# New landing delays in a planner's DMA model, and new orders and placements for attention followed by an MoE layer, on one core

## The chip, the cores and the metric

The kernel runs on one core of a Trainium2 chip. The metric is the device time of one execution in microseconds (us); where several executions were timed, their median is given. The core has five engines with an instruction queue each: TensorE (PE, with its weight loads PEld), VectorE (DVE), ScalarE (ACT), GpSimd (POOL) and SyncE (SP), which here issues every DMA. Each engine works through its own queue in order; engines wait for each other by semaphores.

## What is computed

The input is q, k and v of 4 batches, 8 heads, 576 positions and 64 dimensions, and two weights. Attention is the sum of two parts, one over means of four positions, one over a band of seven:

```python
q_d = q.reshape(B, H, Sd, factor, D).mean(axis=3)   # factor = 4, k_d and v_d alike
out_d = sm_attn(q_d, k_d, v_d)
out_up = np.repeat(out_d, factor, axis=2)
mask = np.abs(pos[:, None] - pos[None, :]) < factor
scores = np.where(mask, scale * np.matmul(q, k.transpose(0, 1, 3, 2)), -1000000000.0)
...
out_local = np.matmul(attn, v)
return (out_up + out_local).astype(np.float32)
```

Its result, as x of 2304 tokens by 512, goes through a layer with weights of 512 by 2048 and 2048 by 512:

```python
h = x @ w_in
sp = np.where(h > 20.0, h, np.log1p(np.exp(np.minimum(h, 20.0))))
g = h * np.tanh(sp)
return (g @ w_out).astype(np.float32)
```

## The kernel before

Attention is cut into 16 units, one for each batch b and pair p of heads (`attention`, line 399; "unit 2_1" is batch 2, pair 1). A unit loads qk (line 417, 582 KB) and vv (line 503, 1152 KB). DVE sums qk over four positions (line 418), PE makes coarse scores (line 433) and banded scores (line 472), ACT takes the exponentials (lines 440 and 482 or 492), DVE divides by their sums. POOL sums v over four positions (lines 506 and 508). PE transposes the probabilities (lines 517, 518, 551) and multiplies them with the sums of v (lines 538 and 542) and with v (line 566). DVE adds both parts into x32 (line 579).

The MoE layer works on 384 tokens (c, six of them) and 128 columns of w_in (f, sixteen of them). Tokens of c = 0 and 1 are split into two float32r parts in SBUF and go through 32 "slots" (line 773): four times three matmuls into h (line 785), then `tail` (line 791): Mish on ACT (line 809), a split into two parts (lines 812 to 815), and nine matmuls into the accumulators (line 828). Tokens of c = 2 to 5 go to DRAM (far, line 592), come back as sums (line 646) and operands (line 666, tile q), and go through 16 "quartets" (line 723), which form four products of two c and two f out of seven smaller ones (line 746). A weight (line 614) comes as raw 64-bit numbers (512 KB each for wi and wo), is converted on ACT and DVE (lines 630 to 634) and split (lines 638 to 641).

The first four units (batch 0) run in a prologue with three buffer sets of their own and a fourth that is shared; matmuls on the identity (line 927, "warm") fill PE's gaps there. All later units share the one set "att", whose buffers exist once: a buffer goes to the next unit in program order when the one before is through (`turn`, lines 82 and 214). The quartets' operands lie in that set too (lines 674, 675 and 707 to 714).

The order of instructions is not written out. Every operation is recorded with an engine, a duration, what it reads and writes, and a priority (a low number is urgent). `Plan.order` (line 173) then plays the whole program through: each time an engine is free by its clock, it gets the most urgent operation whose inputs are there. What comes out is the fixed order of each engine's queue. For SP (lines 270 to 273) it has a model of when a DMA lands: `o.dur` is bytes over 415 GB/s, `dma` the end of what was queued before.

The constants at the top set priorities and choices: ATT (base and step for each batch) with UNIT (one unit) give a unit's priority, ATT[b][0] + ATT[b][1] * p + UNIT; slots have their number s, 0 to 31, and quartets start at 32. LAG puts the second product behind s (three values: s < 20, < 60, above). WPRI (base, step for each f, extra for wo), WACT and WDMA belong to weights, SPRE, SPRE2, JPRE and XDMA to sums, QPRE, QPRE2, QDMA to operands, TPRE and UPRE to quartets, VOFF to vv's DMA; STICK and KEEP make PE and ACT stay with matmul shapes and function tables. AMUL, AEXP, WHI, RDV and GHI list the units, weights and slots for which a step is done on ACT or on DVE: a unit in AMUL normalises on ACT (line 448), else on DVE (line 451); in AEXP it takes nine exponentials with their sums on ACT (line 482), else one, with DVE passes around it (lines 490 to 493); in RDV it spreads the rest of the coarse part on DVE (line 524), else with three ACT operations (line 530).

Of the kernel before, what the change touches and what calls it, by code (L numbers as in the profile page):

```python
# [19 lines left out]
P = 128  # L20
BIG = 1e30
CH = 384
LAG = (0.33, 3.75, 19.55)
FA = 5
SETS = 3
ATT = {0: (-845.5, 70.5), 1: (0.3, 1.8), 2: (-2.6, 0.3), 3: (-13.3, 4.2)}
WPRI = (1.59, 11.3, 10.35)
UNIT = {(0, 0): -48, (1, 3): -18, (0, 3): 15, (1, 2): -6, (0, 2): 17, (1, 1): -23, (0, 1): 65, (1, 0): 8, (3, 3): 14, (2, 3): -12, (3, 2): 5, (2, 0): -3, (2, 2): 6, (3, 0): -11, (2, 1): -3, (3, 1): -23}
WARM = True
NPRO = 4  # L30
WACT = 95
STICK = 71
VOFF = 12
WDMA = -72
PIPE0 = (1, 0, 1)
PIPE1 = (1, 0, 1)
LEAD = 3
PMASK = (0, 1)
AMUL = ((0, 2), (0, 3), (1, 0), (1, 1), (1, 3))
AEXP = ((0, 2), (1, 2))  # L40
WHI = ((0, 'wo'), (4, 'wo'), (7, 'wi'), (8, 'wi'), (12, 'wi'), (12, 'wo'), (13, 'wo'), (14, 'wo'), (15, 'wo'))
RDV = ((0, 1), (0, 2), (0, 3), (1, 3), (2, 2), (2, 3), (3, 0), (3, 1), (3, 2))
GHI = (9, 10, 11, 13, 14, 15, 18, 21, 22, 24, 25, 29, 31)
NMISH = (4,)
TAIL = 0
SPRE = 39
SPRE2 = 77
JPRE = -42
XDMA = -35
QPRE = 26  # L50
QPRE2 = 101
QSTEP = 0.6
QDMA = 93
SUMS = 2
TPRE = 82
UPRE = -19
KEEP = 94
LOAD, PRE = 1320, 250
TICK, BUSY, PACE = 3413.3, 3900, 4900
KW = 38  # L60
RATE, LAND = 415.0, 1100
PAGE, FIRST, FETCH = 256, 193, (2800, 5500)
DQ = 2500
# [33 lines left out]
class Plan:  # L97
# [6 lines left out]
    def buf(self, group, tag, shape, dtype=F32, bufs=1, name=None):  # L104
        return Buf(self, group, tag, shape, dtype, bufs, name or f"{tag}_{len(self.ops)}")
# [67 lines left out]
    def order(self):  # L173
# [10 lines left out]
        free = {"pe": 1500.0, "act": 1900.0, "dve": 0.0, "pool": 3290.0, "sp": 1080.0}  # L184
        dma, hot, parked, gap, look = 0.0, {0: 1000}, {}, 0, 0.0
# [4 lines left out]
        events, t, out = [0.0, *free.values()], 0.0, []  # L190
        while events:
            t = heapq.heappop(events)
            while events and events[0] <= t:
                heapq.heappop(events)
            for e in pending:
                while pending[e] and pending[e][0][0] <= t:
                    o = heapq.heappop(pending[e])[2]
# [4 lines left out]
                if e == "pe" and gap > 0 and ready[e]:  # L202
                    ready[e] = [(o.prio + (0 if o.gap else STICK), o.seq, o) for _, _, o in ready[e]]
                    heapq.heapify(ready[e])
                if e == "act" and ready[e]:
                    ready[e] = [(o.prio + (KEEP if o.tab and o.tab != tab else 0), o.seq, o) for _, _, o in ready[e]]
                    heapq.heapify(ready[e])
                while ready[e]:
                    item = heapq.heappop(ready[e])
                    o = item[2]  # L210
# [57 lines left out]
                        dur += max(0, lock["pool" if e == "dve" else "dve"] - t)  # L268
                        lock[e] = t + dur
                    if e == "sp":  # L270
                        late = t > 1e5
                        dma = max(dma, t + LAND + 400 * late) + o.dur * (1 + 0.28 * late)
                        free[e], end = max(t + 420, dma - DQ), dma + 600 * (late and o.dur < 800)
                    else:
                        free[e] = end = t + dur
                    o.end = end
# [22 lines left out]
                if e == "pe" and self.filler and free[e] <= t:  # L299
                    k = int(t // TICK)  # L300
                    o, when = None, max(1700, t + 120)
                    if 1700 <= t < 1e6 and self.load(t) < PACE:
                        o = self.fill(t)
# [23 lines left out]
def dve(n, fast=False):  # L327
    return 69 + (0.52 if fast else 1.042) * n


def act(n, psum=False, extra=0):
    return (52 if psum else 94) + 0.833 * n + 93 * extra
# [6 lines left out]
class Kernel:  # L339
# [59 lines left out]
    def attention(self, b, p, sb, ps, padded, loose):  # L399
# [45 lines left out]
        op("dve", 88, lambda: nc.vector.reciprocal(cst()[:, 3], cst()[:, 2]), w=[cst], two=False)  # L445
        if (b, p) in AMUL:
            for m in range(3):
# [14 lines left out]

        pmask = b in PMASK or (b, p) in AEXP

# [11 lines left out]
        wide = lambda i: lst()[:, i, :, None].broadcast_to([P, T, KW])  # L476
        if (b, p) in AEXP:
            op("dve", dve(T * KW), lambda: nc.vector.tensor_reduce(out=lst()[:, 0], in_=sl3(), op=ALU.max, axis=AX.X),
# [6 lines left out]
        else:  # L485
            if not pmask:
# [7 lines left out]
               r=[L], w=[lst], two=False)  # L494
        if (b, p) in AEXP:
            op("dve", 73, lambda: nc.vector.tensor_scalar(lst()[:, 1], lst()[:, 1], 1e-9, None, op0=ALU.add), r=[L], w=[lst])
# [3 lines left out]

        pv_ = pl.prio + VOFF
        vv, vd = buf("vv", [P, 18, P]), buf("vd", [P, 2, P])
# [12 lines left out]
        def tr():  # L515
# [6 lines left out]
            AT(), pa()[:, :384].rearrange("p (m h i) -> p h m i", m=3, h=2)[:, :, :, :48], AF.Copy), r=[pa], w=[AT])  # L522
        if (b, p) in RDV:
            op("dve", dve(288), lambda: nc.vector.tensor_tensor(
# [89 lines left out]
    def load_w(self, f):  # L614
# [6 lines left out]
        for nm, src in (("wi", wi), ("wo", wo)):  # L621
            pl.prio = prio + (WPRI[2] if nm == "wo" else 0)
            raw = pl.buf("wa" if f < FA else "wb", f"{nm}{f}", [P, 512, 2], I32, 1, f"raw_{nm}{f}")
# [4 lines left out]
            op("sp", P * 4096 / RATE, lambda raw=raw, src=src: nc.sync.dma_start(  # L628
                raw().rearrange("p (c f) w -> p c (f w)", c=4), src), w=[raw], prio=pl.prio + WDMA)
            op("act", act(512), lambda hi=hi: nc.scalar.activation(  # L630
                hi().bitcast(F32), hi().bitcast(F32), AF.Prelu, scale=2.0 ** -112, alpha=2.0 ** 32), w=[h], prio=pl.prio + WACT, tab="exp")
            op("dve", dve(512, True), lambda lo=lo: nc.vector.tensor_scalar(
# [3 lines left out]
               r=[l, h], w=[full])  # L636
            if (f, nm) in WHI:
                op("dve", dve(512, True), lambda w=w, full=full: nc.vector.tensor_copy(w()[:, 0], full()), r=[full], w=[(w, 0)])
# [7 lines left out]
    def sums(self, c):  # L646
# [4 lines left out]
        for j in range(2):  # L651
            pl.prio = (SPRE if c == 2 else SPRE2) + j * JPRE
            at = {}
            for k, (p, d) in raw.items():
                at[k] = b = pl.buf("stg", "stg", [P, 512], F32, self.nstg, f"s{k}{j}_{c}")
                x = self.far(p + j, c + d)
                op("sp", P * 4 * W / RATE, lambda b=b, x=x: nc.sync.dma_start(b()[:, :W], x()), r=[x], w=[b], prio=pl.prio + XDMA)
            for t, ko, a, b_, alu in ((1, "a22", "a21", "a22", ALU.add), (3, "a21", "a11", "a21", ALU.subtract),
# [4 lines left out]
                x = self.far("s", t, j, c)  # L663
                op("sp", P * 4 * W / RATE, lambda bo=bo, x=x: nc.sync.dma_start(x(), bo()[:, :W]), r=[bo], w=[x], prio=pl.prio + XDMA)

    def operands(self, c):
# [15 lines left out]
        for m, what in enumerate(("00", 2, "20", 3, 1, "21", 4)):  # L682
            for j in range(2):
                pl.prio = (QPRE if c == 2 else QPRE2) + m * QSTEP
                if isinstance(what, str):
                    p, d = int(what[0]) + j, int(what[1])
                    x, to = self.far(p, c + d), self.raw[p, d]
                else:
# [6 lines left out]
                op("sp", P * 4 * W / RATE, lambda b=b, x=x: nc.sync.dma_start(b()[:, :W], x()), r=[x], w=[b, (o, kh), (o, kl)],  # L695
                   prio=pl.prio + QDMA)
                op("act", act(W), lambda b=b, w=w: nc.scalar.activation(w()[:, 0], b()[:, :W], AF.Copy), r=[b], w=[(o, kh)])
# [25 lines left out]
    def quartet(self, s, i, c):  # L723
        nc, pl = self.nc, self.plan
        op = pl.op
        pl.prio = s + TPRE
        T = self.blocks(i)
# [24 lines left out]
        def plus(to, a, bank):  # L752
            op("dve", dve(CH), lambda: nc.vector.tensor_tensor(  # L753
                out=at[to](), in0=bank()[:, :CH], in1=at[a](), op=ALU.add),
               r=[bank] + u[a] * (a != to), w=u[to], prio=s + UPRE, two=False)

        bank = product(0, wt(w0, 0), xs(0, c))
        op("act", act(CH, True), lambda bank=bank: nc.scalar.activation(at["u1"](), bank()[:, :CH], AF.Copy),
           r=[bank], w=u["u1"], prio=s + UPRE)
        plus("u2", "u1", product(1, tt(2), ss(2)))  # L760
# [30 lines left out]
    def tail(self, s, c, f, h, own=None, place=("mish", "g"), last=None):  # L791
# [12 lines left out]
        for c0, c1, key in parts:  # L804
# [5 lines left out]
               r=h_, w=x_, tab="mish")  # L810
            if s in GHI:
                op("dve", dve(n, True), lambda o_=o_: nc.vector.tensor_copy(g()[:, 0, o_], Gv()[:, o_]), r=x_, w=[one])
# [10 lines left out]
        for i in range(3):  # L823
# [7 lines left out]
            gi = [g] if len(parts) == 1 else [(g, 2 * i), (g, 2 * i + 1)]  # L831
            op("pe", 700, mm2, r=[*gi, wo], w=[a_], cols=1536, prio=s + LAG[(s >= 20) + (s >= 60)] - 0.5 + 0.1 * i)
            if not last:
# [12 lines left out]
    def run(self, ctx):  # L846
# [29 lines left out]
        for b in (0, 1):  # L876
            for p in range(self.NPAIR):
                if len(units) == NPRO:
                    break
                units.append((ATT[b][0] + ATT[b][1] * p + UNIT.get((b, p), 0), self.attention(  # L880
                    b, p, sets[len(units) % len(sets)], ("props", "attps"),
# [4 lines left out]
        for f in range(self.NF):  # L886
            pl.prio = WPRI[0] + WPRI[1] * f
            self.load_w(f)
# [10 lines left out]
        def units(bs):  # L899
            us = [(ATT[b][0] + ATT[b][1] * p + UNIT.get((b, p), 0), self.attention(b, p, "att", "attps", probs["att"], False))  # L900
                  for b in bs for p in range(self.NPAIR) if 4 * b + p >= NPRO]
            self.record(us, PIPE1)
# [93 lines left out]
```

## Time and profile before

| what | value |
|---|---|
| median of 3 runs | 502.12 us (501.51 to 505.4) |
| the profiled execution | 505.01 us, its span 503.2 us |
| PE busy | 482.8 us (96%) |
| DVE, ACT, POOL busy | 360.8, 280.5, 40.8 us |
| DMA moved | 65.60 MB, mean 130 GB/s |
| mean granted clock of PE | 0.993 of full speed |
| chain that ended last | PE 79%, DMA 8%, ACT 7%, DVE 3%, POOL 2% |

All times inside the execution count from the start of its span. Busy means that the profile shows at least one instruction of the engine under way. A wait stands with the operation that it delayed, and names the engine, or the transfer, that ended it.

### The profile page before, as it was taken

How to read it: one execution, taken by the hardware profiler on the slowest of the kernel's cores; microseconds unless marked ns; L12 is line 12 of the kernel's file. 1: busy time of each engine (PE TensorE's matmuls, PEld its weight loads, DVE VectorE, ACT ScalarE, POOL GpSimd, SP SyncE). 2: the span in 40 equal slices, each digit the busy share in tenths (PEclk: the TensorE clock that was granted, in tenths of full speed). 3: DMA queues.
4: the chain of work that ended last, by engine and by line, in shares of the span. 5: the costliest groups of instructions: out<-in, count | busy, mean ns of one | idle time of the engine just before them, and what ended most of it. 6: DMA issues, size and time to landing. Idle time of an engine off the chain costs nothing.

```text
span 503.2 us, 11610 instructions
## 1 busy us (share of the span) xinstructions
PE 482.8 (96%) x4729; PEld 415.0 (82%) x4729; DVE 360.8 (72%) x818; ACT 280.5 (56%) x668; POOL 40.8 (8%) x70
## 2 busy tenths in 40 slices
PE   7998899989899999999999999999999999999996
PEld 3666788778788788888899999999889999888885
DVE  3999989979665778746896786667789976653511
ACT  2699899757485568675444333343566444333411
POOL 7401001011120111111000000000000000000000
PEclk9989899999999999999999999999999999999999
DMA  8967994314555478636210140100340000000003
GB/s 343 419 274 290 411 360 161 130 60 175 174 207 177 151 236 267 223 117 214 87 48 21 45 139 18 31 17 15 96 150 23 0 2 2 0 0 1 0 1 125
DMA packets 23381, 65.60 MB, mean 130 GB/s; under 512 B 2592, under 2 KB 12832, under 8 KB 21280
## 3 DMA queue, kind: packets, MB, share of 16 engines
q1 hardware_dynamic: 23328, 64.86, 35.9%
q8 instruction: 37, 0.61, 0.5%
q14 instruction: 16, 0.13, 0.1%
HBM read 53.84 MB, written 11.01 MB: 129 GB/s over the span
## 4 chain that ended last, share of the span: by engine, by line
PE 79%; DMA 8%; ACT 7%; DVE 3%; POOL 2%; issue 1%; POOLq 0%; SPq 0%
PE acc L828 35%; PE h L746 24%; PE h L785 9%; DMA vv<-in_vv_dram 4%; PE pve L566 2%; DMA raw_wi<-in_w_in_dram 2%; PE sc L433 2%; PE sl L472 2%; PE pt L551 1%; DMA far<-x 1%; PE pvo L538 1%; PE pvo L566 1%; POOL vv L506 1%; ACT raw_wi L630 1%; PE pvo L542 1%
## 5 line engine op out<-in xcount | busy, mean ns | idle before, releaser
L828 PE MATMUL acc<-wo,g 128*128 128x512 f32 x864 | 219.1, 395 | 0.5 <-ACT g L814 0.5
L828 PEld LDWEIGHTS acc<-wo,g 128*128 128x128 f32 x864 | 159.2, 188 | 30.0 <-ACT g L814 1.4
L753 DVE TENSOR_TENSOR u<-h,u 128x384 f32<-128x384 f32 x112 | 60.7, 554 | 30.4 <-PE h L746 27.9
L785 PE MATMUL h<-x,wi 128*128 128x384 f32 x384 | 76.6, 347 | 2.9 <-ACT mA L809 2.9
L785 PEld LDWEIGHTS h<-x,wi 128*128 128x128 f32 x384 | 67.8, 192 | 5.8 <-ACT mA L809 3.5
L809 ACT ACTIVATE u<-u 128x384 f32<-128x384 f32 (+1 forms) x66 | 33.8, 515 | 61.8 <-DVE u L753 61.6
L815 DVE TENSOR_TENSOR g<-u,g 128x384 fp32r<-128x384 f32 (+1 forms) x66 | 35.6, 544 | 38.5 <-ACT g L814 38.5
L814 ACT ACTIVATE g<-u 128x384 fp32r<-128x384 f32 (+1 forms) x66 | 33.5, 512 | 30.3 <-PE acc L828 29.4
L718 ACT ACTIVATE t<-b 128x256 fp32r<-128x256 f32 x64 | 26.3, 414 | 42.4 <-PE h L746 37.3
L746 PE MATMUL h<-x,wi 128*128 128x384 f32 x192 | 41.3, 338 | 0.0
L746 PE MATMUL h<-x,t 128*128 128x384 f32 x192 | 39.0, 338 | 0.6 <-DVE u L753 0.6
L506 POOL TENSOR_TENSOR vv<-vv 128x512 f32<-128x512 f32 x16 | 21.0, 1315 | 194.6 <-DMA vv<-in_vv_dram 166.3
L746 PEld LDWEIGHTS h<-x,wi 128*128 128x128 f32 x192 | 34.3, 188 | 1.6
L746 PEld LDWEIGHTS h<-x,t 128*128 128x128 f32 x192 | 33.8, 188 | 2.0 <-DVE u L753 1.2
L746 PE MATMUL h<-sfar,t 128*128 128x384 f32 x144 | 32.0, 340 | 0.1
L418 DVE TENSOR_REDUCE qkd<-qk 128x288 f32<-128x1152 f32 x16 | 21.4, 1340 | 13.4 <-DMA qk<-in_qk_dram 13.2
L719 DVE TENSOR_TENSOR t<-b,t 128x256 fp32r<-128x256 f32 x64 | 26.5, 418 | 4.0 <-ACT t L718 3.7
L746 PEld LDWEIGHTS h<-sfar,t 128*128 128x128 f32 x144 | 25.6, 188 | 3.5 <-DVE u L753 0.8
L715 DVE TENSOR_TENSOR b<-b,b 128x256 f32<-128x256 f32 x64 | 27.0, 423 | 1.0
L815 DVE TENSOR_TENSOR g<-mA,g 128x384 fp32r<-128x384 f32 x32 | 21.1, 665 | 8.7 <-ACT g L814 8.5
L709 DVE TENSOR_TENSOR b<-wi 128x256 f32<-128x256 f32 x64 | 25.8, 424 | 0.9 <-PE pvo L538 0.2
L566 PEld LDWEIGHTS pve<-PT,vv 38*64 38x64 f32 x640 | 21.1, 135 | 3.4 <-ACT PT L558 1.2
(116 smaller groups left out, 687.4 us busy)
## 6 DMA issues: line engine op xcount, KB each, us to landing
vv<-in_vv_dram SPq DMA_DIRECT2D x16, 1152.0 KB, 6.7
qk<-in_qk_dram SPq DMA_DIRECT2D x16, 582.0 KB, 6.6
raw_wi<-in_w_in_dram SPq DMA_DIRECT2D x16, 512.0 KB, 10.7
raw_wo<-in_w_out_dram SPq DMA_DIRECT2D x16, 512.0 KB, 10.4
out_dram<-o SPq DMA_DIRECT2D x18, 256.0 KB, 2.1
sa<-far SPq DMA_DIRECT2D x16, 192.0 KB, 2.8
fars<-sa SPq DMA_DIRECT2D x16, 192.0 KB, 2.8
q<-fars SPq DMA_DIRECT2D x16, 192.0 KB, 3.3
```

The source lines that it names most:

```text
L506: op("pool", gps(512), lambda: nc.gpsimd.tensor_tensor(out=vc()[:, :, 0:2], in0=vc()[:, :, 0:2], in1=vc()[:, :, 2:4], op=ALU.add), w=[(vv, ...
L566: nc.tensor.matmul(o_()[64 * h:64 * h + 64, c0:c0 + 32], vw()[64 * e:64 * e + KW, j, f, 64 * h:64 * h + 64], PT()[64 * e:64 * e + KW, j, 6 ...
L715: op("dve", dve(n), lambda ko=ko, a=a, b_=b_: nc.vector.tensor_tensor(out=t[ko](), in0=t[a](), in1=t[b_](), op=ALU.subtract), r=[t[a], t[b ...
L718: op("act", act(n), lambda w=w, ko=ko: nc.scalar.activation(w()[:, 0], t[ko](), AF.Copy), r=[t[ko]], w=[(w, 0)])
L719: op("dve", dve(n), lambda w=w, ko=ko: nc.vector.tensor_tensor(out=w()[:, 1], in0=t[ko](), in1=w()[:, 0].bitcast(F32), op=ALU.subtract), r ...
L746: nc.tensor.matmul(bank()[:, :CH], wv(a, j), xv()[:, b_], start=j == 0 and m == 0, stop=j == 1 and m == 2)
L753: op("dve", dve(CH), lambda: nc.vector.tensor_tensor(out=at[to](), in0=bank()[:, :CH], in1=at[a](), op=ALU.add), r=[bank] + u[a] * (a != t ...
L785: nc.tensor.matmul(h()[:, :CH], w()[:, a, kt * P:(kt + 1) * P], x()[:, b_, :], start=kt == 0 and j == 0, stop=kt == 3 and j == 2)
L809: op("act", act(n, psum), lambda o_=o_: nc.scalar.activation(Gv()[:, o_], Hv()[:, o_], AF.Mish), r=h_, w=x_, tab="mish")
L814: op("act", act(n), lambda o_=o_: nc.scalar.activation(g()[:, 0, o_], Gv()[:, o_], AF.Copy), r=x_, w=[one])
L815: op("dve", dve(n), lambda o_=o_: nc.vector.tensor_tensor(out=g()[:, 1, o_], in0=Gv()[:, o_], in1=g()[:, 0, o_].bitcast(F32), op=ALU.subtr ...
L828: nc.tensor.matmul(a_(), g()[:, a, i * P:(i + 1) * P], wo()[:, b_], start=first and j == 0, stop=last and j == 2)
```

## The change

Three lines of the planner's DMA model change, and constants at the top of the kernel. Before, a transfer had a start-up of 1100 ns up to 100 us of planned time and 1500 ns after; after 100 us its duration counted 1.28 times, and transfers priced below 800 ns (up to 256 KB) ended 600 ns later. Now the start-up is 1100 ns in the first 3 us and 1800 ns from then on; from 70 us the duration counts 1.28 times, and the 600 ns are added below 800 ns and above 2500 ns, which is vv. The constants give other priorities to units, weights, sums, operands and second products, and other choices between ACT and DVE. No operation is added or taken out but for those choices; the matmuls stay the same.

```diff
--- before.py
+++ after.py
@@ -20,41 +20,41 @@
 P = 128
 BIG = 1e30
 CH = 384
-LAG = (0.33, 3.75, 19.55)
+LAG = (0.1, 6.06, 26.18)
 FA = 5
 SETS = 3
-ATT = {0: (-845.5, 70.5), 1: (0.3, 1.8), 2: (-2.6, 0.3), 3: (-13.3, 4.2)}
-WPRI = (1.59, 11.3, 10.35)
-UNIT = {(0, 0): -48, (1, 3): -18, (0, 3): 15, (1, 2): -6, (0, 2): 17, (1, 1): -23, (0, 1): 65, (1, 0): 8, (3, 3): 14, (2, 3): -12, (3, 2): 5, (2, 0): -3, (2, 2): 6, (3, 0): -11, (2, 1): -3, (3, 1): -23}
+ATT = {0: (-842.3, 62.6), 1: (2.8, 3.8), 2: (-7.2, 5.7), 3: (-35.9, 5.6)}
+WPRI = (-2.33, 7.84, 15.62)
+UNIT = {(0, 0): -55, (1, 3): -15, (0, 3): 10, (1, 2): -8, (0, 2): 23, (1, 1): -38, (0, 1): 67, (1, 0): 5, (3, 3): 8, (2, 3): -11, (3, 2): 0, (2, 0): 2, (2, 2): 12, (3, 0): 2, (2, 1): 5, (3, 1): -22}
 WARM = True
 NPRO = 4
-WACT = 95
-STICK = 71
-VOFF = 12
-WDMA = -72
+WACT = 184
+STICK = 34
+VOFF = 1
+WDMA = -65
 PIPE0 = (1, 0, 1)
 PIPE1 = (1, 0, 1)
 LEAD = 3
 PMASK = (0, 1)
-AMUL = ((0, 2), (0, 3), (1, 0), (1, 1), (1, 3))
-AEXP = ((0, 2), (1, 2))
-WHI = ((0, 'wo'), (4, 'wo'), (7, 'wi'), (8, 'wi'), (12, 'wi'), (12, 'wo'), (13, 'wo'), (14, 'wo'), (15, 'wo'))
-RDV = ((0, 1), (0, 2), (0, 3), (1, 3), (2, 2), (2, 3), (3, 0), (3, 1), (3, 2))
-GHI = (9, 10, 11, 13, 14, 15, 18, 21, 22, 24, 25, 29, 31)
+AMUL = ((0, 2), (1, 0), (1, 1))
+AEXP = ((0, 2),)
+WHI = ((0, 'wo'), (2, 'wo'), (7, 'wi'), (8, 'wi'), (11, 'wi'), (12, 'wi'), (14, 'wo'), (15, 'wi'), (15, 'wo'))
+RDV = ((0, 0), (0, 1), (0, 2), (0, 3), (1, 0), (1, 3), (2, 0), (3, 0), (3, 2), (3, 3))
+GHI = (9, 10, 12, 13, 14, 16, 17, 18, 20, 23, 24, 25, 30)
 NMISH = (4,)
 TAIL = 0
-SPRE = 39
-SPRE2 = 77
-JPRE = -42
-XDMA = -35
-QPRE = 26
-QPRE2 = 101
+SPRE = 44
+SPRE2 = 104
+JPRE = -45
+XDMA = -45
+QPRE = -15
+QPRE2 = 100
 QSTEP = 0.6
-QDMA = 93
+QDMA = 51
 SUMS = 2
-TPRE = 82
-UPRE = -19
-KEEP = 94
+TPRE = 92
+UPRE = -20
+KEEP = 121
 LOAD, PRE = 1320, 250
 TICK, BUSY, PACE = 3413.3, 3900, 4900
 KW = 38
@@ -268,9 +268,9 @@
                         dur += max(0, lock["pool" if e == "dve" else "dve"] - t)
                         lock[e] = t + dur
                     if e == "sp":
-                        late = t > 1e5
-                        dma = max(dma, t + LAND + 400 * late) + o.dur * (1 + 0.28 * late)
-                        free[e], end = max(t + 420, dma - DQ), dma + 600 * (late and o.dur < 800)
+                        late = t > 7e4
+                        dma = max(dma, t + (LAND if t < 3000 else LAND + 700)) + o.dur * (1 + 0.28 * late)
+                        free[e], end = max(t + 420, dma - DQ), dma + 600 * (late and (o.dur < 800 or o.dur > 2500))
                     else:
                         free[e] = end = t + dur
                     o.end = end
```

## Rows read from the trace of the kernel before

**Rows 1.** The page: the span, and busy time of each engine
```profile
span 503.2 us, 11610 instructions
...
PE 482.8 (96%) x4729; PEld 415.0 (82%) x4729; DVE 360.8 (72%) x818; ACT 280.5 (56%) x668; POOL 40.8 (8%) x70
```

**Rows 2.** Busy us by stretch: PE, PEld, DVE, ACT, POOL; clock, DMA share, GB/s
```profile
0.00:42.00 42.00, 35.91 (x813) 23.36 (x813) 32.74 (x80) 26.38 (x91) 15.26 (x46) 0.96 0.81 318
42.00:110.00 68.00, 61.95 (x599) 52.70 (x597) 60.50 (x132) 58.80 (x139) 6.57 (x6) 0.97 0.67 257
110.00:242.00 132.00, 128.16 (x2042) 109.98 (x2042) 95.28 (x215) 86.33 (x201) 18.97 (x18) 1.00 0.55 185
242.00:499.70 257.70, 256.82 (x1293) 228.99 (x1285) 172.24 (x396) 108.64 (x238) 0.00 (x0) 1.00 0.12 37
```

**Rows 3.** Groups by line and shape, PE: the filler
```profile
L927 PE MATMUL warm<-ident 128*128 128x512 bf16 x32 | 11.3, 471 | 1.6 <-POOL ident masks.py:199 1.6
```

**Rows 4.** Timeline of PE: waits between 100 and 242 us, idle before in brackets
```profile
106.15 0.31 PE L518 MATMUL at<-ident,Ar_att 128*96 128x128 f32 x1 [1.63 <-DVE Ar_att L454]
...
138.79 0.47 PE L538 MATMUL pvo<-AT,vd 128*64 128x144 f32 x4 [1.67 <-POOL vd L508]
...
165.40 0.47 PE L538 MATMUL pvo<-AT,vd 128*64 128x144 f32 x4 [0.74 <-POOL vd L508]
...
233.24 2.33 PE L785 MATMUL h<-x,wi 128*128 128x384 f32 x12
...
237.82 0.47 PE L538 MATMUL pvo<-AT,vd 128*64 128x144 f32 x4 [0.89 <-POOL vd L508]
```

**Rows 5.** Timeline of DVE around 105 us
```profile
104.63 1.35 DVE L418 TENSOR_REDUCE qkd<-qk 128x288 f32<-128x1152 f32 x1 [3.11 <-DMA qk<-in_qk_dram]
...
105.90 0.20 DVE L454 TENSOR_TENSOR Ar_att<-A,cst 128x48 f32<-128x48 f32 x1
```

**Rows 6.** Timeline of SyncE's DMA queue: when four transfers were issued
```profile
95.31 0.33 SPq L503 DMA_DIRECT2D vv<-in_vv_dram  x1
...
97.84 0.33 SPq L417 DMA_DIRECT2D qk<-in_qk_dram  x1
...
128.67 0.33 SPq L503 DMA_DIRECT2D vv<-in_vv_dram  x1
...
227.80 0.33 SPq L503 DMA_DIRECT2D vv<-in_vv_dram  x1
```

**Rows 7.** Chain that ended last: start us, us, what; two transfers of vv
```profile
128.67 7.51 DMA vv<-in_vv_dram
...
156.10 6.99 DMA vv<-in_vv_dram
```

**Rows 8.** Timeline of POOL: sums of v behind two transfers
```profile
136.67 1.27 POOL L506 TENSOR_TENSOR vv<-vv 128x512 f32<-128x512 f32 x1 [12.29 <-DMA vv<-in_vv_dram]
...
138.01 0.72 POOL L508 TENSOR_TENSOR vd<-vv 128x256 f32<-128x256 f32 x1
...
235.68 1.29 POOL L506 TENSOR_TENSOR vv<-vv 128x512 f32<-128x512 f32 x1 [16.73 <-PE h L785]
```

**Rows 9.** DMA issues between 100 and 240 us: KB each, median us to landing
```profile
vv<-in_vv_dram SPq DMA_DIRECT2D x9, 1152.0 KB, 6.0
```

**Rows 10.** Groups by line, DVE and ACT: busy us, mean ns, idle before
```profile
L493 DVE TENSOR_REDUCE lst<-L_att 128x9 f32<-128x351 f32 x14 | 7.2, 511 | 0.0
...
L451 DVE TENSOR_TENSOR A<-A,cst 128x384 f32<-128x384 f32 x11 | 6.1, 554 | 0.1
...
L524 DVE TENSOR_TENSOR R_att<-at,diag 96x288 f32<-96x288 f32 x9 | 4.1, 451 | 2.0 <-ACT AT L521 1.8
...
L448 ACT ACTIVATE A<-A,cst 128x128 f32<-128x128 f32 x15 | 5.2, 398 | 0.2 <-DVE cst L445 0.2
...
L482 ACT ACTIVATE L_att<-sl,lst 128x38 f32<-128x38 f32 x18 | 5.2, 300 | 0.7 <-DVE lst L480 0.6
```

**Rows 11.** Waits of PE: us in total, times, longest
```profile
PE h L785 <- ACT mA L809: 2.9, 2, 2.3
```

## The prediction

> **What bounds the kernel now.** I read the page's first part, then the busy times by stretch, then the waits of TensorE (PE) in order of time, and then went back from each wait to the transfer behind it. PE is busy for 482.8 of 503.2 us; no other engine is above 72% [rows 1]. The stretches say where the other 20.4 us are [rows 2]: 6.1 in the first 42 us, where PE waits on chains of VectorE (DVE) and ScalarE (ACT) and partly runs filler; 6.05 between 42 and 110; 3.8 between 110 and 242; 0.9 in all of the last dense part up to 499.7; and 3.5 after PE's last instruction, for the last output. So the second half (the quartets) can give nothing: 256.8 of its 257.7 us are PE work that the change leaves alone. Whatever it does, it does before 242 us, and there out of 16 us of idle PE, plus the 11.3 us of filler [rows 3].
>
> The waits themselves [rows 4]: one of 1.63 us at 106.15 for a DVE operation, three of 1.67, 0.74 and 0.89 us in front of the matmuls at line 538 for GpSimd's (POOL's) sum of v. The first one looks like a matter of DVE but isn't. DVE stood idle for 3.11 us in front of its reduction of qk, for a DMA, and the operation that PE needs (line 454) is right behind it in DVE's queue [rows 5]. That qk transfer was issued at 97.84, behind a vv transfer of 95.31 [rows 6] and one of the output copies to DRAM (far); DVE could start at 104.63, so qk took 6.8 us. The three later ones are plainly vv: issued at 128.67 [rows 6], under way for 7.51 us, and 6.99 us for the one of 156.10 [rows 7]; POOL then needs 2.1 us for its two sums before PE may go on [rows 8]. The one of 227.80 let POOL start 7.9 us later, at 235.68 [rows 6, 8].
>
> **The change, part by part.** *The model.* Every engine's order is fixed before the run by the planner's own clock, and each engine then works through its order without overtaking; so a transfer that lands later than the planner thought stops its engine although other work was there. The planner prices a vv at 1,179,648 bytes / 415 = 2.84 us. In the old model, up to 100 us, it lands 1.10 + 2.84 = 3.94 us after issue, after that 1.50 + 1.28 x 2.84 = 5.14. In the new one, from 70 us on, it is 1.80 + 3.64 + 0.60 = 6.04. The trace has a median of 6.0 us for the nine vv between 100 and 240 us [rows 9]: on the mean the new figure is right and the old one 0.9 short.
>
> Now each wait. At 95.31 the old model had vv at 99.25, the far transfer (96 to 192 KB, 0.24 to 0.47 us) behind it and qk (1.44 us) at about 101.0. DVE waited until 104.6, so the plan was 3.6 us wrong. The new one has the data at 100.75, far at 101.1 to 101.4 and qk at 102.9 to 103.2, which takes back 2.0 of the 3.6. As PE lost 1.63 us of it, less than 2.0, I take the wait of 1.63 as gone: the planner will put other slots' matmuls there. At 138.79 PE waited 1.67; the model moves by 0.90, so 0.77 stays. At 165.40 (0.74) and 237.82 (0.89) the 0.90 covers the whole wait. Sum: 1.63 + 0.90 + 0.74 + 0.89 = 4.16 us. What covers these gaps is matmul work of MoE slots (lines 785 and 828), which PE has to do anyway and which is there: a unit's vv is issued about every 14 us and PE is otherwise full [rows 2]. What would be late next is the rest of the landing delay, the 1.5 us that the new model still lacks at 128.67. Bounds: nothing is gained if the delays fall elsewhere in the new plan; 4.93 if all four go, the 0.77 with them.
>
> A vv of 1152 KB took 6.0 us in the median and 7.51 and 6.99 us in two that PE waited for [rows 7, 9]. The Trainium skill, DMA: Bandwidth & Descriptors, section "Anatomy of one DMA — SWDGE (gpsimd) path", gives a fixed cost of about 2.0 us plus bytes at 436 GB/s (for another issuing path than SyncE's); an estimate from it is 4.7 us. By that the old 5.14 was long enough and the new 6.04 would only put line 538 later, for no gain; the rows disagree with it, and the measurement decides.
>
> Early transfers (3 to 70 us) get 0.7 us more start-up, without the longer rates. There the planner's queue is mostly backed up, and its formula then counts rate only, so I take nothing; bounds 0 to 0.7 us once.
>
> *Order and placement.* The units of batches 1 to 3 share one set of buffers whose turns follow the program, so units 1_0 to 3_3 stay in that order, and those of batch 0 still sort as 0, 1, 2, 3 (priorities -897, -713, -694, -645 against -894, -710, -688, -619). What moves is how urgent units are against slots. Batch 3 goes from -24, -32, 0, 13 to -34, -52, -25, -11, so it is pulled forward; batch 2 from -6, -5, 4, -14 to -5, 4, 16, -1, so it is put back a little. Each unit's DMAs, POOL sums and output transfers move along on SP's and POOL's queues; POOL has room (19 of 132 us between 110 and 242 [rows 2]), SP holds back only what it issues. I take 0 for the placement itself, because PE's work is the same and its idle there is already priced; bounds from the rest of the idle between 42 and 242 (9.9 - 4.2 = 5.7 us gained) down to a loss in the rival below.
>
> *Engine choices.* Units 0_3 and 1_3 leave AMUL (three ACT operations of 398 ns each become one on DVE of 554 ns [rows 10]), 1_2 leaves AEXP (nine exponentials of 0.30 us become one over all 342 elements, taken like DVE's 0.51, and DVE gets two more passes of 0.51 us for some small operations [rows 10]), and 0_0 and 1_0 join RDV (451 ns on DVE each [rows 10]). DVE gains 1.11 + about 0.7 + 0.90 = 2.7 us in the first 110 us, ACT loses 2.4 + 2.2 us and the small copies. DVE has 7.5 us idle between 42 and 110, ACT 9.2 [rows 2]; so I take 0. If no cover is left, it costs 2.7; if ACT was what PE waited for, it gives up to the 2.9 us of waits on ACT's mish [rows 11].
>
> *The rest.* Weights get the order wi0, wi1, wo0 instead of wi0, wo0, wi1; LAG holds the second product back longer from slot 20 on; q tiles are loaded earlier. The last two act in a part with 0.9 us of idle: 0, bounded by that 0.9 below and by the 3.8 us of the stretch before above.
>
> **Sum.** The profiled execution took 505.01 us, its span 503.2, the other 1.8 us lying outside. 505.01 - 4.16 = 500.85. The median of the three runs, 502.12, is 2.89 us lower, so the same saving gives 502.12 - 4.16 = 498.0 us, 0.8% less. A measurement of this kernel can tell about 1%, 5 us, from no change; the forecast lies inside that, near its edge.
>
> **Rivals.**
> A, the forecast, 498.0, 42%, own range 496 to 500.5.
> B, the new order also takes ACT's waits: 4.6 us less work for ACT and mish with the weights put behind it. For it: ACT is busy 58.8 of 68 us between 42 and 110 [rows 2], and the two waits on mish cost 2.9 us [rows 11]. Against it: DVE, busy 60.5 us there, gets the work, and the early rates in the model are unchanged. 498.0 - 2.9 = 495.1; with a quarter of the filler gone too, 492.3. 28%.
> C, the delay is no constant: it comes from transfers queued before it (the 16 DMA engines are busy 55% between 110 and 242 [rows 2]; 5.14 planned against 6.0 and 7.51), and a new order has its late ones elsewhere, so as much waits as before: 502. The skill's rule above ends here too. 13%.
> D, slower: the chain of attention ends last. vv has one buffer; its next transfer starts only when the unit before has finished. If each of the eight units of batches 2 and 3 has its line 538 placed 0.90 us later, the row of units grows by 7.2 us, and the quartets cannot start, since their operands lie in the same buffers. It decides when slots run out before the last unit: now the last first-product of a slot starts at 233.24 and the last unit's line 538 only at 237.82 with 0.89 us of waiting [rows 4], so it is near. Against it: batch 3 is made more urgent. 502.12 - 4.16 + 7.2 = 505.2; if the three vv waits stay as well, 507.7. 17%.
>
> **How the numbers follow.** Predicted 498.0. Low 493.5 and high 505.5 leave out B's far end (about 8%) and D's (about 11%). Faster by over 1% (under 497.1): B's 28% and 10 of A's 42, together 0.38. Within 1%: 32 of A, C's 13 and 7 of D, 0.52. Slower (over 507.1): 10 of D, 0.10.
>
> **What would show it.** Right: the waits of PE on POOL's line 508 fall from 3.3 us to under 1, DVE's wait for qk near 100 us shrinks by about 2, PE idle between 110 and 242 falls under 2 us, quartets start 3 to 5 us earlier, and from there the stretch is as long as now. B: waits on mish gone and the first MoE matmul before 42 us. C: as many us on vv or qk at other places. D: the first quartet product comes later than now, behind a vv. Wrong altogether: if PE's busy time itself moves by more than 3 us, or the last stretch changes in length.

## The result and the profile after

The changed kernel takes 497.26 us in the median of 7 runs (496.62 to 499.04), the kernel before 503.53 in the median of 7 (501.51 to 509.85). The ratio is 0.9887, 95% interval 0.9858 to 0.9916: 5.7 us less, where 4.2 were forecast. The ratio is one of means and leaves out the run of 509.85 us, a slow one. 497.26 lies within the range. The saving is just past the 1% that counts as faster, for which the forecast gave 38%, but the interval reaches back under 1%, to which it gave 52%.

The page of the changed kernel, span and busy times, against [rows 1]:

```profile
span 495.5 us, 11601 instructions
...
PE 479.5 (97%) x4728; PEld 412.8 (83%) x4728; DVE 361.2 (73%) x821; ACT 281.2 (57%) x642; POOL 43.5 (9%) x70
```

The span is 7.7 us shorter than in the profiled execution before. PE was idle for 20.4 us there and is for 16.0 now; its busy time fell by 3.3 us as well. To see where, I cut both executions at the first matmul of a slot (42.38 us before, 42.65 after), at 112 us, and at the first matmul of a quartet on the operand sfar (248.48 before, 240.44 after). The first and the last of these cuts are the same place in the work: behind the last, PE has 1243 matmuls left in both (xN counts instructions). Busy us by stretch: PE, PEld, DVE, ACT, POOL, then the granted clock of PE, DMA share and GB/s; the kernel before:

```profile
42.38:112.00 69.62, 63.41 (x610) 54.15 (x611) 62.12 (x136) 59.73 (x142) 6.57 (x6) 0.98 0.65 249
112.00:248.48 136.48, 132.85 (x2066) 113.99 (x2065) 98.27 (x222) 88.17 (x205) 18.97 (x18) 1.00 0.53 181
```

The changed kernel:

```profile
0.00:42.65 42.65, 35.03 (x813) 22.95 (x814) 33.36 (x81) 25.53 (x86) 15.60 (x46) 0.96 0.79 316
42.65:112.00 69.35, 66.06 (x783) 56.50 (x784) 66.64 (x144) 61.42 (x135) 9.20 (x8) 1.00 0.74 281
112.00:240.44 128.44, 127.70 (x1892) 109.68 (x1891) 94.48 (x214) 87.36 (x192) 18.70 (x16) 1.00 0.52 176
240.44:492.00 251.56, 250.68 (x1243) 223.65 (x1241) 166.72 (x385) 106.53 (x232) 0.00 (x0) 1.00 0.11 37
```

The prologue is as long as before (+0.27). From sfar to the end of the span it is 503.2 - 248.48 = 254.7 us before and 495.5 - 240.44 = 255.1 after: nothing. Everything lies between: 206.1 us before, 197.8 after, 8.3 less. Of these, 5.8 are PE's idle time: 6.2 + 3.6 = 9.84 before, 3.3 + 0.7 = 4.03 after (stretch less PE busy). The waits of PE now (us in total, times, longest), of which the rows on mish answer to [rows 11] and the row on POOL to [rows 4]:

```profile
PE h L785 <- ACT mA L809: 1.4, 2, 1.2
PE h L785 <- DVE wi L641: 1.0, 1, 1.0
...
PE at L517 <- DVE A L451: 0.7, 1, 0.7
...
PE pvo L538 <- POOL vd L508: 0.4, 1, 0.4
```

The waits on POOL's vd fell from 3.3 us (1.67 + 0.74 + 0.89) to 0.43, the wait at line 518 is gone, the waits on mish went from 2.9 to 1.4, and 1.0 on DVE's weights and 0.7 on its normalising at line 451 are new. The reduction of qk that DVE waited 3.11 us for in [rows 5] begins at 93.21 now, without a wait. DVE's longest wait for qk between 60 and 112 us is now

```profile
77.56 1.35 DVE L418 TENSOR_REDUCE qkd<-qk 128x288 f32<-128x1152 f32 x1 [1.85 <-DMA qk<-in_qk_dram]
```

Another of 2.93 us remains at 152.45, and PE doesn't wait for it.

Another 1.7 us is PE's clock. Here are the stretches 56:60, 60:62 and 62:64 of the kernel before, with the granted clock in the third column from the right:

```profile
56.00:60.00 4.00, 1.73 (x11) 1.45 (x10) 3.72 (x9) 3.44 (x6) 0.00 (x0) 0.95 1.03 412
60.00:62.00 2.00, 2.00 (x8) 2.00 (x8) 1.77 (x4) 2.00 (x6) 0.00 (x0) 0.50 1.03 412
62.00:64.00 2.00, 2.00 (x9) 1.91 (x9) 2.00 (x5) 0.64 (x2) 0.00 (x0) 0.74 1.02 408
```

and of the changed kernel:

```profile
56.00:60.00 4.00, 4.00 (x24) 3.88 (x23) 3.93 (x9) 4.00 (x8) 0.00 (x0) 1.00 1.03 410
60.00:62.00 2.00, 1.82 (x16) 1.09 (x14) 1.97 (x6) 1.98 (x4) 0.00 (x0) 1.00 1.05 418
62.00:64.00 2.00, 0.94 (x5) 0.94 (x6) 2.00 (x6) 1.99 (x5) 0.00 (x0) 1.00 1.00 401
```

Before, PE had been idle for 2.3 us up to 59.59, and was granted 0.95, then 0.50 (1.2 GHz), then 0.74; the time lost is 4 x 0.05 + 2 x 0.50 + 2 x 0.26 = 1.7 us. The changed kernel was idle for a shorter 1.23 us near 62, and the clock stayed at 1.00 (2.4 GHz). PE's busy time between the cuts fell by 2.5 us, 196.3 to 193.8, and these 1.7 are part of it; 5.8 + 1.7 leaves 0.8 us of the 8.3 that no row names.

The transfers themselves land about as the new model has them: the eight vv issued between 100 and 240 us have a median of 5.7 us to landing, against 6.0 in [rows 9]. Two of them on SP's queue, the second being the last vv, then POOL's starts behind them, then PE:

```profile
158.44 0.34 SPq L503 DMA_DIRECT2D vv<-in_vv_dram  x1
...
220.25 0.33 SPq L503 DMA_DIRECT2D vv<-in_vv_dram  x1
```

```profile
164.46 1.30 POOL L506 TENSOR_TENSOR vv<-vv 128x512 f32<-128x512 f32 x1 [12.27 <-DMA vv<-in_vv_dram]
...
227.79 1.29 POOL L506 TENSOR_TENSOR vv<-vv 128x512 f32<-128x512 f32 x1 [15.41 <-DMA vv<-in_vv_dram]
```

```profile
226.32 1.22 PE L746 MATMUL h<-x,wi 128*128 128x384 f32 x6
227.37 2.88 PE L828 MATMUL acc<-wo,g 128*128 128x512 f32 x12
230.19 0.47 PE L538 MATMUL pvo<-AT,vd 128*64 128x144 f32 x4
```

The first took 6.0 us from issue to POOL's start, which is the new model's 6.04. The last took 7.5 us, as long as those that held PE before (7.51 in [rows 7], 7.9 in [rows 6, 8]), and still PE doesn't wait at line 538: six matmuls of a quartet and twelve of slots' second products now stand in front of it. So this wait went because of what stands before line 538; the transfer itself is still 1.5 us behind the new model's figure. The last unit loads 7.6 us earlier than in [rows 6], and the first quartet product starts at 226.32, before that unit is through; in the kernel before it starts at 239.76.

### The profile page after: what moved, and what is told of

It is laid out like the page before. It is cut to its first block, busy times and chain, and to the rows that moved or that the text cites. A ratio compares the mean times of both kernels' runs of the same rounds, so it can differ in the third digit from the quotient of the medians.

```text
span 495.5 us, 11601 instructions
## 1 busy us (share of the span) xinstructions
PE 479.5 (97%) x4728; PEld 412.8 (83%) x4728; DVE 361.2 (73%) x821; ACT 281.2 (57%) x642; POOL 43.5 (9%) x70
## 4 chain that ended last, share of the span: by engine, by line
PE 81%; ACT 9%; DVE 7%; issue 2%; POOL 1%; ACTq 0%; DVEq 0%; POOLq 0%
PE acc L828 37%; PE h L746 24%; PE h L785 9%; PE sc L433 2%; PE pve L566 2%; PE sl L472 2%; PE pt L551 1%; ACT raw_wi L630 1%; ACT L809 1%; PE pvo L538 1%; ACT raw_wo L630 1%; PE at L517 1%; DVE qkd L418 1%; ACT mA L809 1%; ACT A L440 1%
## 5 line engine op out<-in xcount | busy, mean ns | idle before, releaser
L785 PE MATMUL h<-x,wi 128*128 128x384 f32 x384 | 75.6, 344 | 2.4 <-ACT mA L809 1.4
L785 PEld LDWEIGHTS h<-x,wi 128*128 128x128 f32 x384 | 66.0, 188 | 5.6 <-ACT mA L809 2.1
L506 POOL TENSOR_TENSOR vv<-vv 128x512 f32<-128x512 f32 x16 | 22.8, 1423 | 184.0 <-DMA vv<-in_vv_dram 144.1
L746 PE MATMUL h<-x,wi 128*128 128x384 f32 x192 | 38.7, 337 | 0.0
L746 PEld LDWEIGHTS h<-x,wi 128*128 128x128 f32 x192 | 34.1, 188 | 1.0
L815 DVE TENSOR_TENSOR g<-mA,g 128x384 fp32r<-128x384 f32 x32 | 18.3, 581 | 9.9 <-ACT g L814 9.7
L440 ACT ACTIVATE A<-sc,cst 128x144 f32<-128x144 f32 x48 | 18.0, 379 | 12.0 <-DVE cst L438 11.9
```

What stands on the lines that cost most here:

```text
L746: nc.tensor.matmul(bank()[:, :CH], wv(a, j), xv()[:, b_], start=j == 0 and m == 0, stop=j == 1 and m == 2)
L785: nc.tensor.matmul(h()[:, :CH], w()[:, a, kt * P:(kt + 1) * P], x()[:, b_, :], start=kt == 0 and j == 0, stop=kt == 3 and j == 2)
L815: op("dve", dve(n), lambda o_=o_: nc.vector.tensor_tensor(out=g()[:, 1, o_], in0=Gv()[:, o_], in1=g()[:, 0, o_].bitcast(F32), op=ALU.subtr ...
```

## The experiments

What has to be told apart is the cause. The forecast had it that the three new lines of the model remove the waits, and that the constants are worth nothing by themselves. Ratios are to the kernel before, each timed beside it.

**The model alone.** Only the three lines of the model are new.

```diff
-                        late = t > 1e5
...
+                        late = t > 7e4
...
```

> The kernel before with the three new lines of the DMA model alone; all constants as before. Theory M (the landing delays in the model took the waits away): PE's waits on vd and on qk's DMA fall from about 5 us to about 1, ratio about 0.99. Theory C (the gain comes from the constants, which were chosen anew for the new model): 1.00 or slower, since the old constants were chosen for the old model, the vd waits may fall but as much waiting appears elsewhere. Theory R (every new plan lands somewhere within a few us, whatever caused it): anything from 0.99 to 1.02, no more and no less than a plan moved by a meaningless change.

506.08 us, ratio 1.0035 (0.9997 to 1.0073): no gain. Its busy times by stretch, cut in the same way, and the waits of PE that matter:

```profile
42.69:112.00 69.31, 64.34 (x758) 53.65 (x759) 66.98 (x142) 67.30 (x153) 7.18 (x6) 1.00 0.67 259
112.00:247.66 135.66, 131.06 (x1914) 111.85 (x1914) 95.49 (x214) 84.97 (x195) 20.03 (x18) 1.00 0.53 178
```

```profile
PE h L785 <- ACT mA L809: 2.2, 4, 1.2
PE pvo L538 <- POOL vd L508: 1.8, 1, 1.8
PE at L517 <- DVE A L451: 1.8, 2, 1.2
...
PE h L746 <- ACT t L718: 1.2, 1, 1.2
...
PE at L518 <- DVE Ar_att L454: 0.7, 1, 0.7
```

The lines did what they should to the waits that the forecast counted: vd from 3.3 to 1.8, line 518 from 1.63 to 0.7. But PE's idle in the two stretches is 5.0 + 4.6 = 9.57 us, as good as the 9.84 of before: DVE's normalising (line 451, 1.8) and one vv, for which POOL waited 6.6 us from its issue, hold PE now, beside ACT's mish. Behind sfar ACT's half of a quartet's weight block (line 718) holds it for another 1.2. Two waits on DVE, 1.19 us at 92.75 (line 451) and 0.72 at 116.40 (line 454), come behind operations of DVE that began while POOL was summing v:

```profile
89.73 1.32 POOL L506 TENSOR_TENSOR vv<-vv 128x512 f32<-128x512 f32 x1 [11.68 <-DMA vv<-in_vv_dram]
...
114.68 1.60 POOL L506 TENSOR_TENSOR vv<-vv 128x512 f32<-128x512 f32 x1 [22.50 <-DMA vv<-in_vv_dram]
```

```profile
89.90 1.70 DVE L634 SCALAR_TENSOR_TENSOR full_wo<-raw_wo 128x512 int32<-128x512 int32 x1
...
115.08 1.27 DVE L454 TENSOR_TENSOR Ar_att<-A,cst 128x48 f32<-128x48 f32 x1
```

At other times of this trace line 634 takes 0.69 us and line 454 0.19; here both end only behind POOL's sum (by 0.5 and 0.1 us). The clock stayed at 1.00 in both stretches, and from sfar to the end it took 2 us longer. The time is that of rival C of the prediction, but its mechanism, as many us on vv or qk at other places, is shown for a part only: vd's 1.8 us, and 0.6 us for a sum of qk (line 418), where 4.9 had been.

**The constants alone.** The changed kernel with the old three lines.

```diff
-                        late = t > 7e4
...
+                        late = t > 1e5
...
```

> The changed kernel with the three old lines of the DMA model; all constants new. Theory M: the waits on vd and qk return, 4 to 5 us slower than the changed kernel, ratio to before about 0.998. Theory C: stays near the changed kernel, ratio about 0.99. Theory R: 0.99 to 1.02.

500.88 us, ratio 0.9915 (0.9882 to 0.9947). Under the old model the new constants keep most of the gain, 4.3 of 5.7 us by the ratios; the interval overlaps that of the changed kernel, so what the lines add on top is not resolved. Its two stretches:

```profile
42.65:112.00 69.35, 65.34 (x770) 55.40 (x771) 64.78 (x146) 63.93 (x133) 8.02 (x7) 1.00 0.72 280
112.00:239.57 127.57, 125.50 (x1887) 107.50 (x1886) 94.70 (x212) 85.77 (x194) 20.05 (x18) 1.00 0.53 178
```

Idle 4.0 + 2.1 = 6.08 us; 1.1 us of it are waits on vd. (Its sfar comes early, at 239.57, because 18 matmuls more than in the changed kernel are left behind it.) Theory C was nearest in both runs, theory M wrong in both.

**Is every new plan a throw of the dice?** A change of 10 ns in the start-up says nothing of the chip, but gives another order. In the kernel before, and in the changed one:

```diff
-RATE, LAND = 415.0, 1100
+RATE, LAND = 415.0, 1110
```

> The kernel before with 10 ns more on the start-up of every transfer in the planner's model (1110 for 1100), a change that says nothing about the chip but makes the planner's order another one from about 45 us on. Theories M and C: 10 ns are nothing, the time stays within 2 us of before, ratio 0.997 to 1.005. Theory R: the plan that was found for exactly the old numbers is lost, 2 to 8 us slower, ratio 1.004 to 1.016.

> The changed kernel with the same 10 ns more. Theories M and C: as the changed kernel, ratio to before 0.986 to 0.992. Theory R: 2 to 8 us slower than the changed kernel, ratio 0.993 to 1.005.

506.66 us, 1.0027 (1.0001 to 1.0053), and 499.25 us, 0.9884 (0.9851 to 0.9917). These two disturbances cost 0.3% or nothing; theory R had 1.004 to 1.016 for the first and 0.993 to 1.005 for the second. The second is clearly outside, the first interval reaches into it. The test is a weak one. By the traces PE's order in the kernel before is another from 48 us on, but ACT's and DVE's only from about 140 us, and in the changed kernel only from about 189 us. So up to 112 us, where half of the saved idle time lies, the order of ACT and DVE was not disturbed at all, and it is one disturbance of each plan. The gain doesn't hang on the last 10 ns, but it is not excluded that another choice of constants would have done as well; the searches below bear on that.

**One group of constants at a time,** in the kernel before: the lists of what runs on ACT or DVE; the placement of attention; the weights. And the changed kernel with the old lists.

```diff
-AMUL = ((0, 2), (0, 3), (1, 0), (1, 1), (1, 3))
+AMUL = ((0, 2), (1, 0), (1, 1))
...
```

> The kernel before with only the new lists of which step runs on ACT or DVE (AMUL, AEXP, WHI, RDV, GHI); priorities and model old. Theory W (work that moved from ACT to DVE is what helps, since ACT with its Mish held PE between 42 and 112 us): ratio 0.990 to 0.995, waits on mish down. Theory P (the new priorities, attention placed anew among the slots, are what helps): 1.00 or slower. Theory J (the constants help only together): 1.00 to 1.01.

```diff
-AMUL = ((0, 2), (1, 0), (1, 1))
+AMUL = ((0, 2), (0, 3), (1, 0), (1, 1), (1, 3))
...
```

> The changed kernel, model and priorities new, with the old lists of steps on ACT or DVE. Theory W: back to 0.998 to 1.005, waits on mish of 2 us or more. Theory P: keeps 0.988 to 0.993. Theory J: 1.00 to 1.01.

```diff
-ATT = {0: (-845.5, 70.5), 1: (0.3, 1.8), 2: (-2.6, 0.3), 3: (-13.3, 4.2)}
+ATT = {0: (-842.3, 62.6), 1: (2.8, 3.8), 2: (-7.2, 5.7), 3: (-35.9, 5.6)}
...
-VOFF = 12
+VOFF = 1
```

> The kernel before with only the new placement of attention (ATT, UNIT, VOFF). Theory P: ratio 0.988 to 0.994, with the waits on vd under 1.5 us. Theory W and theory J: 0.997 to 1.01.

```diff
-WPRI = (1.59, 11.3, 10.35)
+WPRI = (-2.33, 7.84, 15.62)
-WACT = 95
+WACT = 184
-WDMA = -72
+WDMA = -65
```

> The kernel before with only the new priorities of weights (WPRI, WACT, WDMA). If the order of weights is what removed the 2.3 us wait near 60 us and the low clock behind it: ratio 0.993 to 0.997 and a granted clock of 1.00 between 60 and 64 us. Theories P, W and J: 0.998 to 1.01.

Lists 1.0008 (0.9983 to 1.0032), attention 1.0012 (0.9985 to 1.0039), weights 1.011 (1.0064 to 1.0157), all but the lists 1.0293 (1.025 to 1.0336). None of these three groups brings anything alone; weights alone cost 1.1%, and the changed kernel without its lists is slower than the kernel before by 2.9%, which no theory had. Theories W and P fall; J, that they help only together, is what is left, though its 1.00 to 1.01 missed that run. The other constants (LAG, STICK, KEEP and those of sums, operands and quartets) and pairs of groups were not run. Three stretches of the last one, and the waits of PE in the first of them:

```profile
140.00:170.00 30.00, 25.31 (x336) 20.14 (x335) 15.64 (x34) 18.90 (x46) 4.21 (x4) 0.89 0.45 153
170.00:200.00 30.00, 29.90 (x465) 26.16 (x465) 16.78 (x37) 18.72 (x40) 4.42 (x4) 1.00 0.51 171
...
230.00:258.85 28.85, 24.69 (x476) 19.35 (x475) 22.04 (x54) 14.31 (x42) 4.46 (x4) 0.99 0.54 180
```

```profile
143.94 0.55 PE L517 MATMUL at<-ident,A 128*128 128x128 f32 x3 [1.29 <-DVE A L451]
...
146.44 3.17 PE L828 MATMUL acc<-wo,g 128*128 128x512 f32 x6 [1.32 <-ACT g L814]
...
163.62 1.32 PE L785 MATMUL h<-x,wi 128*128 128x384 f32 x6 [2.00 <-ACT mA L809]
```

PE is idle for 4.7 us between 140 and 170, for 1.29 on DVE, 1.32 on ACT's half of g and 2.00 on its mish, and its clock falls to 0.89 there. The new priorities were chosen for the split of work between DVE and ACT in the new lists; that this is why they fail without it is an argument from these waits, not a test.

**What is a better model worth in choosing constants?** The order is a product of constants and model, so I let the constants be searched anew, by small random changes that were kept where the planner's own end came earlier: from the old constants under the new model, from the old constants under the old one, and on from the new constants under the new. A fourth kernel is the changed one again. The first of them begins:

```diff
-LAG = (0.33, 3.75, 19.55)
+LAG = (-0.27, 3.53, 28.33)
...
-AMUL = ((0, 2), (0, 3), (1, 0), (1, 1), (1, 3))
+AMUL = ((0, 2), (0, 3), (1, 0), (1, 1), (1, 3), (2, 0), (2, 3), (3, 2), (3, 3))
...
```

> The kernel before with the new DMA model, and its constants searched anew from the old ones: some 12,000 small random changes, each kept where the planner's own end came earlier. Theory Q (what the model is worth is the choice of constants that it allows: a plan that is short by a truer clock is short on the chip): ratio 0.983 to 0.992, like the changed kernel. Theory S (any further search helps, under whatever model): the same as n_oldmodel. Theory L (the changed kernel's constants were a lucky draw): 0.998 to 1.01.

> The same search with as many changes, from the same old constants, under the old DMA model. Theory Q: no gain on the chip, ratio 0.997 to 1.008, with PE waiting for vd or qk again. Theory S: 0.983 to 0.992. Theory L: 0.998 to 1.01.

> The changed kernel, its constants searched on in the same way under the new model. If the planner's clock is true to within 1 us, 1 to 2 us faster than the changed kernel: ratio 0.983 to 0.987. If what is left between planned and real time is larger than that, about the changed kernel, 0.986 to 0.993.

> The changed kernel once more, beside the three searched ones on the same chip: 0.986 to 0.992 by its first measurement.

New model 0.9913 (0.9885 to 0.9942), old model 0.9946 (0.9914 to 0.9979), on from the changed kernel 0.9840 (0.9797 to 0.9884), the changed kernel again 0.9853 (0.9810 to 0.9896). Searching from the old constants helps under either model, 0.9% and 0.5%; the intervals overlap, and it is one search under each, so neither Q nor S is settled. Theory L falls in so far as another search under the new model gained nearly as much as the changed kernel. The search on from the changed kernel, 497.13 us beside 497.69, is not clearly faster than it. Its two stretches, with those of the changed kernel's second execution the fullest of all:

```profile
42.61:112.00 69.39, 66.68 (x786) 56.93 (x787) 66.06 (x145) 60.84 (x132) 9.25 (x8) 1.00 0.73 281
112.00:239.58 127.58, 127.12 (x1888) 109.12 (x1888) 87.32 (x204) 86.05 (x203) 17.69 (x16) 1.00 0.53 177
```

Put side by side, time goes with PE's idle time from the first slot on: up to the first use of sfar (the two stretches, each less PE busy), and behind it to the end of the span:

| kernel | ratio to before | PE idle up to sfar, us | behind sfar, us | waits on vd, us |
|---|---|---|---|---|
| searched on from the changed one | 0.9840 | 3.2 | 4.4 | 0.3 |
| changed, again | 0.9853 | 3.2 | 4.4 | 0 |
| changed, 10 ns more | 0.9884 | 4.1 | 4.9 | 0 |
| changed | 0.9887 | 4.0 | 4.4 | 0.4 |
| old constants searched, new model | 0.9913 | 6.4 | 4.4 | 0.2 |
| new constants, old model | 0.9915 | 6.1 | 5.1 | 1.1 |
| old constants searched, old model | 0.9946 | 6.1 | 4.4 | 1.6 |
| before | 1 | 9.8 | 4.4 | 3.3 |
| new lists alone | 1.0008 | 8.3 | 5.0 | 0.6 |
| new attention alone | 1.0012 | 8.9 | 5.1 | 1.6 |
| before, 10 ns more | 1.0027 | 9.2 | 5.7 | 1.4 |
| new model alone | 1.0035 | 9.6 | 5.6 | 1.8 |
| new weights alone | 1.011 | 10.8 | 4.9 | 2.0 |
| changed with old lists | 1.0293 | 13.5 | 5.5 | 0.5 |

The order is not strict: the kernel before and the four rows below it lie within 0.35% of each other. The idle times are those of one execution each, and the clock and the prologue are not in them.

The waits on vd alone don't order the kernels: the last row has 0.5 us of them.

## Why the prediction was right, and where its reasons failed

**Where time can go.** Right: the quartets gave nothing, and all of the gain lies before the first use of sfar, most of it out of PE's idle time there.

**The named waits.** Right as an outcome: 4.16 us were to go, and 4.5 went. The 1.63 are gone, and so are all three named waits on vd, 3.30 in all; one new wait of 0.43 came at 78.44.

**Their cause.** Wrong. The step that failed is that the model's 0.9 us take these waits away while placement counts 0 and slots are there to fill the gaps. With the model alone vd still costs 1.8 us, PE waits on DVE and ACT instead, and the ratio is 1.0035. Nor did the gain need the lines: the new constants under the old model have 1.1 us of vd waits and a ratio of 0.9915. And the last vv of the changed kernel is still 7.5 us under way, 1.5 more than the new model's figure, without a wait of PE.

**Order, lists and weights at 0.** For two of them it holds alone, 1.0008 and 1.0012; as terms to be added it does not. Weights alone cost 1.1%, and without the lists the new order costs 2.9%. These are no terms of a sum: the planner makes one order out of all of them. The sum also left out, without a reason, WHI, GHI, STICK, KEEP and the moves of batches 2 and 3 in RDV. ACT's 4.6 us less work did not come either: ACT is busy for 280.5 us before and 281.2 after. Its function tables are loaded 38 times instead of 34, at 1.28 us each; the four more cost 5.1 us.

**What was not priced.** The 1.7 us of PE's clock behind the longest wait, and about half of the waits on mish (2.9 to 1.4), which had been put under rival B. Less the new waits of 1.0 and 0.7, they make up roughly what 5.7 us is above 4.2. That a sum with a wrong cause, and with these terms left out, ended 0.7 us from the measured 497.26 is in part luck. B itself, with the mish waits and some of the filler gone, did not come whole: the prologue is as long as before.

**The other rivals.** D did not come; the last vv is issued 7.6 us earlier, as the more urgent batch 3 had spoken for. C gives the time of the model without the constants, and its reason for a part of it.

**The signs.** Those for right came: 0.43 us on POOL, no wait for qk near 100 us, 0.74 us of idle PE between 110 and 242 us, and 254.7 against 255.1 us from sfar on. Quartets start earlier by more than the 3 to 5 us that were named: 13.4 us for the first product, 8.0 for sfar. One sign for "wrong altogether" came too: PE's busy time moved by 3.3 us, more than 3. The prologue has 1.2 of it, against 1.5 us more idle time there; the stretches behind it have 2.5, of which the clock is 1.7. The forecast took PE's busy time as fixed, and the clock was not in it.

**What stays open.** Why these constants fit together isn't shown beyond the idle time that they leave. That the truer model is what found them is plausible, 0.9% against 0.5% in the two searches, but not resolved.

## What to carry to other kernels

A better number in a planner's model is worth what the order made with it is worth: change it and choose the constants anew, and judge the whole plan, since single parts of it can cost more than they bring. Price a new plan by the idle time of the engine that bounds the stage, all causes together, and not by the waits that have a name in the old trace; a filled wait is paid only if nothing else is late behind it. To see whether a small gain is more than the luck of an order, disturb the plan by something meaningless and time that, and look in the traces how far the order really changed.

## What the runs showed that was not expected

The prologue is not the same from one execution to the next. The changed kernel's two profiled executions reached the first slot at 42.65 and at 43.30 us. The kernel before with 10 ns more has the same order on every engine up to its first slots, but these began at 45.01 us and not at 42.38. Its prologue, and its longest wait there (idle before in brackets; "issue": for nothing that the profile shows):

```profile
0.00:45.01 45.01, 37.62 (x813) 24.40 (x813) 33.17 (x80) 26.71 (x92) 15.23 (x46) 0.92 0.76 300
```

```profile
27.96 0.24 PE L566 MATMUL pvo<-PT,vv 38*64 38x32 f32 x2 [1.70 <-issue]
```

The granted clock was 0.92 and not 0.96, and the wait before the matmul at line 566, which was 0.88 us in the profile of before, was 1.70. These 2.6 us are nearly half of the gain, so the stretches behind the prologue say more on a plan than single spans do.

A wait can have a second price, and its length alone doesn't say whether. 2.3 us of idle PE near 59 us were followed by 1.7 us lost to the clock, the 1.23 us of the changed kernel by none. But the old constants searched under the old model lost as much (granted 0.82, 0.50 and 0.82 in the six us from 50 on) behind only 1.42 us, and the new attention alone lost nothing behind 2.49. The wait and a stretch behind it, first of the one, then of the other:

```profile
50.25 0.31 PE L518 MATMUL at<-ident,Ar_att 128*96 128x128 f32 x1 [1.42 <-DVE Ar_att L454]
```

```profile
52.00:54.00 2.00, 2.00 (x8) 2.00 (x8) 2.00 (x5) 2.00 (x5) 0.00 (x0) 0.50 1.02 418
```

```profile
61.80 2.35 PE L785 MATMUL h<-x,wi 128*128 128x384 f32 x12 [2.49 <-ACT mA L809]
```

```profile
62.00:64.00 2.00, 2.00 (x13) 2.00 (x13) 1.76 (x4) 2.00 (x7) 0.00 (x0) 1.00 1.04 414
```

What decides it is not shown here.
